# One index for four output rows: table columns in a new order, and a block's four slots in one buffer

## The chip, the cores and the metric

The kernel runs on one core of one Trainium2 chip. The time is the device time of one execution in microseconds (us). The kernel before took 394.58 us as the median of three runs (394.48 to 395.24).

## The reference

The input `x` has 8 sequences of 3072 rows with 256 values. A Fourier transform along the rows and one along the values is taken, and its real part goes through a maxout layer with three weight matrices and an output matrix:

```python
X = np.fft.fft(np.fft.fft(x, axis=1), axis=2).real      # (8, 3072, 256)
h = np.maximum(np.maximum(X @ w1, X @ w2), X @ w3)      # (24576, 768)
out = h @ w_out                                          # (24576, 256), float32
```

The real part at row k and at row 3072 - k consists of the same even and odd parts, added or subtracted. So a kernel can compute rows 0 to 1536 of a sequence and get the others, the mirror rows, from the same operands.

## The kernel before

The work goes in 8 batches, one for each sequence. A batch has two stages.

The first stage (class `Mix`) makes the two matrices `tE` and `tO`, 128 x 1536 each: the even and the odd part of the transform for 1536 output rows, one row of the output for each column. The input lies in `xt`, loaded by GpSimd's queue (`load_x`, L127; `fetch` in the plan) and mirrored (`mirror`). Method `s` transforms along 32 residues, `y` and `z` turn the result over through DRAM (stores of `tb` to `db`, loads of `yb`, both on SP's queue), and `k` (L461 to L471) multiplies with the tables `te_tab` and `to_tab`: one call for each table and each group of 512 columns. The columns of one call belong to several residues r of the row number modulo 32, and each residue needs its own weights (`col`). So a call is as many matmuls as the helper `_parts(g)` lists, 6 for groups 0 and 1 and 8 for group 2. The tables themselves are made once at the start: `ramp` and three more iotas write the row number of each column into `kvec`, and `phase`, `turns`, `wrap`, `angle` and `table` turn it into sines. `m.c` copies the first column of a few residues into `yb`. Row 0 of `tO` goes to DRAM and comes back to all 128 partitions as `vb` (`k` and `v`, SP's queue).

The second stage takes the 1536 columns as 3 blocks of 512 and, for each block, 6 units (one for each 128 of the 768 hidden values; 18 units a batch, 144 in all). A unit computes the three products for the direct rows (`begin`) and, by adding `gd_all` products on the same PSUM, for the mirror rows (`finish`, matmul L497), and takes their maximum into `hp` and `hm`. From unit 7 on, every odd unit is "split": its third product comes from `third` (L815 to L828), where VectorE makes `even` (L824), ScalarE makes `odd`, and GpSimd makes `plus` and `minus` (L828). VectorE's maximum in the split units (L837 for `plus`, L849 for `minus`) waits for these. `third` of a unit is issued one to two units ahead.

The output layer of a block (`l2_block`) runs beside the next block's units: ten matmuls of it are issued after each unit (`l2_some(10)`). A block has four slots of 128 columns. For each slot PE fills one PSUM bank `po` with the direct rows in its first half and the mirror rows in its second, and VectorE adds the even part and writes the 128 x 512 tile `ot` (L541). There are six such tiles. The column order is such that a slot's columns are consecutive values of j for one or two residues, with row number 32 j + r; a slot's direct rows are 32 apart, and `_runs(slot)` gives two or three runs of partitions that each go out with one store on SP's queue (L549), 1 KB a row. The mirror rows of a slot go out with one indexed store on GpSimd's queue (`scatter`, L622), one index and 1 KB a partition; slot 11 leaves out its first partition and stores 127 rows. A `memset` of one value follows each of them (L626). The indices `rows_m` (128 x 96) are made once by `rows`.

The last block of the last batch (`l2_last`) has flipped operands, so that its mirror rows too can leave with plain stores. It takes its slots in the order 3, 0, 1, 2, and after each slot its stores are dealt to ScalarE's, SP's and GpSimd's queues (L584). The row 1536 of all sequences comes from `l2_mid`.

Each engine takes its instructions in the order written here (the schedule is manual). The loop at the end of the kernel writes, for each unit: `finish` of the unit before if it is split, `begin`, `third`, `scatter`, `l2_some(10)`, then what the plan (`at`) holds for this unit. So on GpSimd's queue the indexed stores that have become ready stand between the `minus` of one `third` and the `plus` of the next.

Of the kernel before, what the change touches and what calls it, by code (L numbers as in the profile page):

```python
# [29 lines left out]
def _runs(slot):  # L30

    if slot == 11:
        return [(0, 48, 0), (48, 96, 16), (96, 128, 15 + 32 * 64)]
    t, u = divmod(slot, 3)
    edge, r = 96 - 32 * u, 4 * t + 1 + u
    return [(0, edge, r + 32 * 32 * u), (edge, 128, r + 1)]


def _parts(g):

    cols = [(r, 96 * (r - 1), 96 if r < 15 else 64, 0) for r in range(1, 16)]
    cols += [(0, 1408, 48, 0), (16, 1456, 48, 0), (15, 1504, 32, 64)]
    done = []
    for (r, c, wd, _) in cols:
        a, z = max(c, 512 * g), min(c + wd, 512 * g + 512)
        if a < z:
            done.append(((r - 1) % 16 if r < 16 else 16, a - 512 * g, z - a))
    return done
# [3 lines left out]
def kernel(  # L52
# [62 lines left out]
    rows_m = consts.tile([128, 12 * B], INT32, tag="rows_m")  # L115
# [50 lines left out]
    kvec = gen.tile([128, NHALF + 1], FP32, tag="kvec")  # L166
    kv = kvec[:, 0:1440].rearrange("p (r j) -> p r j", j=96)

    def ramp(r):
        n = {0: 6, 6: 5, 11: 4}[r]  # L170
        iota(kv[:, r:r + n, :], [[1, n], [32, 96]], base=r + 1)

    dvec = gen.tile([128, 128], FP32, tag="dvec")
    for c, (s0, s1) in enumerate(FIRST):
        for h in range(2):
            load_x(0, s0, s1, h)
        if c == 0:
            iota(dvec, [[1, 128]])
        elif c < 3:
            ramp((0, 6)[c - 1])  # L180
# [12 lines left out]
    ramp(11)  # L193
    iota(kvec[:, 1408:1504].rearrange("p (r j) -> p r j", r=2), [[16, 2], [32, 48]])
    iota(kvec[:, 1504:NHALF], [[32, 32]], base=15 + 32 * 64)
    iota(kvec[:, NHALF:NHALF + 1], [[0, 1]], base=NHALF)
# [72 lines left out]
    q = gen.tile([128, NHALF + 1], FP32, tag="q")  # L269
# [118 lines left out]
    class Mix:  # L388
# [72 lines left out]
        def k(self, which, g, evict=nc.scalar.copy):  # L461
# [3 lines left out]
            for (i, c0, wd) in _parts(g):  # L465
                nc.tensor.matmul(ps2[:, c0:c0 + wd], self.col(i, which),  # L466
                                 tab[:, g * 512 + c0:g * 512 + c0 + wd], start=True, stop=True)
# [42 lines left out]

    def l2_hidden(po, hcols):
        for jc in range(NJC):
            nc.tensor.matmul(po, hcols(jc), wout_bf[:, jc * 256:(jc + 1) * 256],  # L513
                             start=False, stop=(jc == NJC - 1), skip_group_check=True)
            yield

    def l2_block(b, blk, hp, hm, te, to):

        base = b * S
        for sub in range(4):  # L520
# [3 lines left out]
            if sub % 2 == 0:  # L524
# [10 lines left out]
            ot = out_pool.tile([128, 512], FP32, name="ot", tag="ot")  # L535
# [6 lines left out]
                out=ot.rearrange("p (h c) -> p h c", h=2),  # L542
                in0=po.rearrange("p (h c) -> p h c", h=2),
                in1=lin.unsqueeze(1).to_broadcast([128, 2, 256]), op=ALU.add)
            lo = 1 if slot == 11 else 0
            waiting.append((b * 12 + slot, lo, ot))
            for (p0, p1, k0) in _runs(slot):
                row = base + k0
                stored(nc.sync.dma_start(out=out[row: row + 32 * (p1 - p0 - 1) + 1: 32, :],  # L549
                                         in_=ot[p0:p1, 0:256]), "direct", ("scattered",))  # L550

    def l2_last(hp, hm, te, to, flipped):

        base = (B - 1) * S
        ter, tor = flipped
        for sub in (3, 0, 1, 2):
# [4 lines left out]
            ot = out_pool.tile([128, 512], FP32, name="ot", tag="ot")  # L561
            for (h, tev, tov, wo, hid) in (
                    (0, te[:, cp], to[:, cp], gw[:, 256:512], lambda jc: hp[:, jc, sp]),
                    (1, ter[:, sm], tor[:, sm], gw[:, 512:768], lambda jc: hm[:, jc, sm])):
                if h == 0 or sub == 2:
# [7 lines left out]
                if sub == 2:  # L573
                    nc.vector.tensor_copy(out=ot[:, h * 256:(h + 1) * 256], in_=ph)
            if sub != 2:
                nc.vector.tensor_copy(out=ot, in_=po)
            stores = [(p0, p1, base + k0, 0) for (p0, p1, k0) in _runs(slot)]
            for (p0, p1, k0) in _runs(slot):
                if k0 == 0:
                    p0, k0 = 1, 32  # L580
                stores.append((128 - p1, 128 - p0, base + S - k0 - 32 * (p1 - p0 - 1), 256))
            for k, (p0, p1, row, c) in enumerate(stores):
                eng = (nc.scalar, nc.sync, nc.gpsimd)[(k + (sub == 2)) % 3]
                stored(eng.dma_start(out=out[row: row + 32 * (p1 - p0 - 1) + 1: 32, :],  # L584
                                     in_=ot[p0:p1, c:c + 256]), "direct", ("scattered",))

    def l2_mid():
# [20 lines left out]
        for _ in l2_hidden(po[0:B, 0:256], lambda jc: hmid[:, jc, :]):  # L608
            pass
        ot = out_pool.tile([128, 512], FP32, name="ot", tag="ot")  # L610
        nc.vector.tensor_copy(out=ot[0:B, 0:256], in_=po[0:B, 0:256])
        stored(nc.sync.dma_start(out=out[NHALF: NHALF + S * (B - 1) + 1: S, :],
                                 in_=ot[0:B, 0:256]), "direct", ("scattered",))
# [4 lines left out]
    def scatter():  # L618

        while waiting:  # L620
            at_row, lo, ot = waiting.pop(0)
            stored(nc.gpsimd.indirect_dma_start(  # L622
                out, bass.IndirectOffsetOnAxis(
                    ap=rows_m[0:128 - lo, at_row: at_row + 1], axis=0),
                ot[lo:128, 256:512], None), "scattered", ("scattered", "direct"))
# [61 lines left out]
    m.c(1, 7)  # L687
# [9 lines left out]
    def rows():  # L697

        rows_f = gen.tile([128, 12 * B], FP32, tag="rows_f")
        iota(rows_f.rearrange("p (b t u) -> p b t u", t=4, u=3), [[S, B], [-4, 4], [-1025, 3]],  # L700
# [224 lines left out]
```

## Time and profile before

| | before |
|---|---|
| median of 3 runs | 394.58 us (394.48 to 395.24) |
| the profiled execution | 395.75 us, span 393.8 us |
| granted TensorE clock | 0.996 |
| TensorE (PE) busy | 377.7 us, 96% |
| VectorE (DVE) busy | 315.0 us, 80% |
| ScalarE (ACT) busy | 263.0 us, 67% |
| GpSimd (POOL) busy | 332.9 us, 85% |
| indexed stores L622 | 92, mean 1113 ns |
| DMA packets, bytes | 66901, 54.20 MB |

In the profile a line like "L622 POOL DMA_INDIRECT out_dram<-ot" names the line of the kernel, the engine, the operation, what is written and what is read. In the order of time the first two numbers are the start and the duration in us, and the brackets hold how long the engine was idle before and what released it. In the chain (the work that ended last, followed back) the numbers are start and length of a link. "issue" is time in which the engine waited for nothing that the profile shows. Matmuls overlap: each has some 0.16 us of latency, and the distance between starts is what a stream of them costs.

### The profile page before, as it was taken

To read this page: it belongs to the slowest core of one execution; us is meant where nothing else is said; L and a number is where in the kernel's file an instruction comes from. 1 tells how busy PE (TensorE), PEld (TensorE's weight loads), DVE (VectorE), ACT (ScalarE), POOL (GpSimd) and SP (SyncE) were. 2 spreads that over 40 slices of the span, in tenths; PEclk is the share of its full clock that TensorE was granted. 3 is DMA by queue.
4 is the path that set the end of the run, shared out by engine and by line. 5 is a ranking of instruction groups with operands and counts; after the bars stand their busy time and mean duration, and the time that the engine had idled before them with its cause. 6 is when DMAs were issued, how large, how long until landed. Compare 5 with 4: busy or idle time off the path is not lost.

```text
span 393.8 us, 8383 instructions
## 1 busy us (share of the span) xinstructions
PE 377.7 (96%) x2710; PEld 235.9 (60%) x2759; DVE 315.0 (80%) x530; ACT 263.0 (67%) x476; POOL 332.9 (85%) x432
## 2 busy tenths in 40 slices
PE   6698999999999999999999999999999999999994
PEld 2354566566665666565665666556665666666673
DVE  7788897788687788788787888877887887887972
ACT  6877788677766887577867787578866447435420
POOL 8985698979978899889988899889977898869993
PEclk9999999999999999999999999999999999999998
DMA  7999576585838776495767876495333553321234
GB/s 115 159 194 183 131 191 146 114 191 150 161 102 144 190 153 144 117 206 137 137 150 120 210 132 160 118 206 124 108 108 101 131 147 90 94 77 47 90 96 131
DMA packets 66901, 54.20 MB, mean 138 GB/s; under 512 B 32702, under 2 KB 62556, under 8 KB 66003
## 3 DMA queue, kind: packets, MB, share of 16 engines
q0 software_dynamic: 24368, 26.53, 35.5%
q1 hardware_dynamic: 41978, 26.72, 27.0%
q8 instruction: 21, 0.34, 0.4%
q10 hardware_dynamic: 512, 0.43, 0.4%
q14 instruction: 22, 0.18, 0.1%
HBM read 36.95 MB, written 30.81 MB: 172 GB/s over the span
## 4 chain that ended last, share of the span: by engine, by line
PE 84%; DMA 4%; DVE 4%; ACT 3%; issue 2%; POOL 2%; SPq 1%; DVEq 0%; ACTq 0%; POOLq 0%
PE po L513 30%; PE pse L497 12%; PE pse L490 8%; PE pse L491 7%; PE po L536 4%; PE d L821 4%; PE pse L835 4%; PE e L819 3%; PE ps L466 3%; PE pse L836 3%; PE pl L528 2%; PE ps L401 2%; DMA yb<-db 2%; DMA xt<-in_x_dram 2%; ACT tb L405 1%
## 5 line engine op out<-in xcount | busy, mean ns | idle before, releaser
L503 ACT ACTIVATE stmp<-pse 128x512 bf16<-128x512 f32 x150 | 89.6, 600 | 66.1 <-PE pse L497 50.9
L622 POOL DMA_INDIRECT out_dram<-ot,rows_m x92 | 102.4, 1113 | 17.9 <-issue 8.8
L828 POOL TENSOR_TENSOR plus<-even,odd 128x512 bf16<-128x512 f32 x69 | 87.8, 1272 | 32.9 <-DVE even L824 32.7
L828 POOL TENSOR_TENSOR minus<-even,odd 128x512 bf16<-128x512 f32 x69 | 87.5, 1268 | 0.0
L513 PE MATMUL po<-wout_bf,hp 128*128 128x256 bf16 x576 | 86.1, 273 | 0.4
L837 DVE SCALAR_TENSOR_TENSOR hp<-pse,plus 128x512 bf16<-128x512 f32 x69 | 47.6, 689 | 46.5 <-PE pse L836 13.9
L513 PE MATMUL po<-wout_bf,hm 128*128 128x256 bf16 x576 | 78.6, 273 | 0.0
L513 PEld LDWEIGHTS <-hp 128*128 128x128 bf16 x576 | 56.4, 98 | 26.1
L497 PE MATMUL pse<-tO,gd_all 128*128 128x512 bf16 x217 | 70.5, 379 | 1.1 <-DVE hp L504 0.2
L513 PEld LDWEIGHTS <-hm 128*128 128x128 bf16 x576 | 56.4, 98 | 16.3
L541 DVE TENSOR_TENSOR ot<-po,even 128x512 f32<-128x512 f32 x92 | 62.7, 681 | 0.0
L504 DVE TENSOR_TENSOR hp<-pse,stmp 128x512 bf16<-128x512 f32 x75 | 51.4, 685 | 10.1 <-ACT stmp L503 8.7
L490 PE MATMUL pse<-tE,g_all 128*128 128x512 bf16 x148 | 56.0, 379 | 1.9 <-DVE tE L468 0.5
L504 DVE TENSOR_TENSOR hm<-pse,stmp 128x512 bf16<-128x512 f32 x75 | 51.5, 687 | 7.4 <-ACT stmp L503 4.1
L824 DVE SCALAR_TENSOR_TENSOR even<-vb,wcol,e 128x512 f32<-128x512 bf16 x69 | 50.8, 737 | 0.0
L491 PE MATMUL pse<-tO,g_all 128*128 128x512 bf16 x131 | 49.6, 379 | 0.2 <-issue 0.2
L849 DVE SCALAR_TENSOR_TENSOR hm<-pse,minus 128x512 bf16<-128x512 f32 x69 | 47.0, 681 | 0.7
L823 ACT ACTIVATE odd<-d 128x512 f32<-128x512 f32 x69 | 41.3, 598 | 6.2
L134 ACT COPY xt<-xt 64x762 bf16<-64x762 bf16 (+1 forms) x48 | 40.2, 838 | 1.1
L497 PEld LDWEIGHTS <-gd_all 128*128 128x128 bf16 x219 | 21.3, 97 | 22.2 <-issue 4.1
L536 PE MATMUL po<-gw,tO 128*128 128x512 bf16 x85 | 32.3, 380 | 0.0
L405 ACT CAST tb<-ps 128x512 bf16<-128x512 f32 x38 | 20.5, 588 | 14.1 <-PE ps L401 14.1
(175 smaller groups left out, 475.7 us busy)
## 6 DMA issues: line engine op xcount, KB each, us to landing
xt<-in_x_dram POOLq DMA_DIRECT2D x14, 384.0 KB, 8.4
out_dram<-ot SPq DMA_DIRECT2D x55, 96.0 KB
out_dram<-ot SPq DMA_DIRECT2D x64, 64.0 KB
db<-tb SPq DMA_DIRECT2D x21, 192.0 KB
vb<-vd SPq DMA_DIRECT2D x23, 128.0 KB
xt<-in_x_dram POOLq DMA_DIRECT2D x7, 400.0 KB, 6.9
xt<-in_x_dram POOLq DMA_DIRECT2D x7, 368.0 KB, 6.1
out_dram<-ot SPq DMA_DIRECT2D x62, 32.0 KB
```

The costliest lines, as they stand in the source:

```text
L490: nc.tensor.matmul(pse[:, 0:n], g_all[:, jc, 2 * i, :], te, start=True, stop=False)
L491: nc.tensor.matmul(pse[:, 0:n], g_all[:, jc, 2 * i + 1, :], to, start=False, stop=True)
L497: nc.tensor.matmul(pse, gd_all[:, jc, i, :], to, start=False, stop=True, skip_group_check=True)
L503: nc.scalar.activation(out=stmp[:, 0:n], in_=pses[0][:, 0:n], func=AX.Relu)
L504: nc.vector.tensor_tensor(out=dst, in0=src3, in1=stmp[:, 0:n], op=ALU.max)
L513: nc.tensor.matmul(po, hcols(jc), wout_bf[:, jc * 256:(jc + 1) * 256], start=False, stop=(jc == NJC - 1), skip_group_check=True)
L536: nc.tensor.matmul(po, to[:, cp], gw[:, 256:768], start=True, stop=True)
L541: nc.vector.tensor_tensor(out=ot.rearrange("p (h c) -> p h c", h=2), in0=po.rearrange("p (h c) -> p h c", h=2), in1=lin.unsqueeze(1).to_br ...
L622: stored(nc.gpsimd.indirect_dma_start(out, bass.IndirectOffsetOnAxis(ap=rows_m[0:128 - lo, at_row: at_row + 1], axis=0), ot[lo:128, 256:51 ...
L824: nc.vector.scalar_tensor_tensor(out=even3, in0=vb, scalar=wcol[:, jc:jc + 1], in1=e3, op0=ALU.mult, op1=ALU.add)
L828: nc.gpsimd.tensor_tensor(out=dst, in0=even3, in1=odd3, op=op)
L837: nc.vector.scalar_tensor_tensor(out=dst, in0=pse2, scalar=0.0, in1=sums[g][0], op0=ALU.max, op1=ALU.max)
```

## The change

The columns of the tables get a new order. A block's four slots now hold four neighbouring residues on the same partition: in block 0, partition c below 96 of slot s holds row 32 c + 4 + s; in block 1 it holds 32 c + 8 + s; in block 2 it holds 32 c + 1 + s for three slots, and row 16 c + 16 in the fourth. Partitions 96 to 127 of every block hold rows 12 + s + 32 (c - 96) + 1024 times the block's number. So four direct rows of one partition are neighbours in the output. `_parts` follows: four pieces of 32 columns, and three or four of 96; in group 2 the fourth slot's 96 columns are two pieces of 48 that take every second column. Groups 0, 1 and 2 now have 8, 8 and 9 matmuls. `_runs` is gone.

A block's four slots go into one buffer of 128 x 8 x 256 values: the direct halves in places 0 to 3 and the mirror halves in places 7 to 4, so that the mirror rows too lie in the order of the output. There are three such buffers: the new `obuf`, and the two halves of `kq`, which holds `kvec` and `q` while the tables are made. The six `ot` tiles are gone.

When all four slots of a block are done, the direct rows leave with two stores on SP's queue in blocks 0 and 1 and three in block 2, up to 4 KB a partition. The mirror rows leave by one indexed store in blocks 0 and 1, of 4 KB for each of 128 indices, and by three in block 2: 96 indices of 3 KB, 32 of 4 KB and 95 of 1 KB. An index now counts groups of four rows, and an element offset gives the first row. `rows_m` has 5 columns, since the batch is in the offset.

`l2_last` takes its slots in the order 1, 2, 3, 0 and stores three of them together after the third, and the two halves of slot 0 as they come. `l2_mid` stores row 0 instead of row 1536 (that is now the column outside the blocks) and takes its tile from `even_pool`. `m.c(1, 7)` and `m.c(7, 16)` become one call before the first `k`; `rows` moves behind the plan's other entries of its unit group.

```diff
-def _runs(slot):
...
+FIRST_OF = (4, 8, 1)
 def _parts(g):
-    cols = [(r, 96 * (r - 1), 96 if r < 15 else 64, 0) for r in range(1, 16)]
-    cols += [(0, 1408, 48, 0), (16, 1456, 48, 0), (15, 1504, 32, 64)]
...
+    done = [(12 + i - 1, slice(128 * i + 96, 128 * i + 128)) for i in range(4)]
+    for i in range(4 if g < 2 else 3):
+        done.append((FIRST_OF[g] + i - 1, slice(128 * i, 128 * i + 96)))
+    if g == 2:
+        done += [(16, slice(384, 480, 2)), (15, slice(385, 480, 2))]
     return done
...
-    def ramp(r):
-        n = {0: 6, 6: 5, 11: 4}[r]
-        iota(kv[:, r:r + n, :], [[1, n], [32, 96]], base=r + 1)
+    def ramp(g):
+        kv = kvec[:, 512 * g:512 * g + 512].rearrange("p (s c) -> p s c", s=4)
+        n = 4 if g < 2 else 3
+        iota(kv[:, 0:n, 0:96], [[1, n], [32, 96]], base=FIRST_OF[g])
+        iota(kv[:, :, 96:128], [[1, 4], [32, 32]], base=12 + 1024 * g)
+        if g == 2:
+            iota(kv[:, 3, 0:96], [[16, 96]], base=16)
+            iota(kvec[:, NHALF:NHALF + 1], [[0, 1]], base=0)
...
+    obufs = [t.rearrange("p (f c) -> p f c", c=256)
+             for t in (obuf, kq[:, 0:2048], kq[:, 2048:4096])]
+    fours = out.rearrange("(n q) d -> n (q d)", q=4)
+    def stores_plus(b, blk, buf, s0=0, s1=4):
+        mine, v = rows_of(b)
+        r, n = FIRST_OF[blk], s1 if blk < 2 else min(s1, 3)
+        yield v[0:96, r + s0:r + n, :], buf[0:96, s0:n, :]
+        yield v[32 * blk:32 * blk + 32, 12 + s0:12 + s1, :], buf[96:128, s0:s1, :]
+        if n < s1:
+            yield mine[16:NHALF + 1:16, :], buf[0:96, 3, :]
+    def stores_minus(b, blk, buf):
+        flat = buf.rearrange("p f c -> p (f c)")
+        if blk < 2:
+            return [(b * S + 1, blk, 0, 128, flat[:, 1024:2048])]
+        return [(b * S + 1, 2, 0, 96, flat[0:96, 1280:2048]),
+                (b * S + 1, 3, 0, 32, flat[96:128, 1024:2048]),
+                (b * S, 4, 0, 95, flat[0:95, 1024:1280])]
...
     def l2_block(b, blk, hp, hm, te, to):
+        buf = obufs.pop(0)
+        obufs.append(buf)
...
             nc.vector.tensor_tensor(
-                out=ot.rearrange("p (h c) -> p h c", h=2),
+                out=buf[:, sub:8 - sub:7 - 2 * sub, :], in0=po.rearrange("p (h c) -> p h c", h=2),
...
-            waiting.append((b * 12 + slot, lo, ot))
-            for (p0, p1, k0) in _runs(slot):
...
+        for (dst, src) in stores_plus(b, blk, buf):
+            store(nc.sync, dst, src)
+        waiting.extend(stores_minus(b, blk, buf))
...
     def l2_last(hp, hm, te, to, flipped):
-        for sub in (3, 0, 1, 2):
+        for sub in (1, 2, 3, 0):
...
+                if sub == 0:
+                    nc.vector.tensor_copy(out=buf[:, 7 * h, :], in_=ph)
+                    stores = (stores_turned(B - 1, buf, 0, 1) if h else
+                              stores_plus(B - 1, 2, buf, 0, 1))
+                elif h:
+                    nc.vector.tensor_copy(out=buf[:, sub:8 - sub:7 - 2 * sub, :],
+                                          in_=po.rearrange("p (h c) -> p h c", h=2))
+                    if sub == 3:
+                        stores = [*stores_plus(B - 1, 2, buf, 1, 4),
+                                  *stores_turned(B - 1, buf, 1, 4)]
+                for k, (dst, src) in enumerate(stores):
+                    store((nc.scalar, nc.sync, nc.gpsimd)[k % 3], dst, src)
...
     def scatter():
         while waiting:
-            at_row, lo, ot = waiting.pop(0)
+            row, col, p0, p1, src = waiting.pop(0)
             stored(nc.gpsimd.indirect_dma_start(
-                out, bass.IndirectOffsetOnAxis(
-                    ap=rows_m[0:128 - lo, at_row: at_row + 1], axis=0),
-                ot[lo:128, 256:512], None), "scattered", ("scattered", "direct"))
+                fours, bass.IndirectOffsetOnAxis(ap=rows_m[p0:p1, col:col + 1], axis=0),
+                src, None, element_offset=256 * row), "scattered", ("scattered", "direct"))
             nc.gpsimd.memset(mark, 0.0)
```

More of the change, by code (lines that the diff above doesn't have):

```diff
@@ L464, in k @@
             ps2 = ps_f.tile([128, 512], FP32, name="ps2", tag="ps")
[L465 to L467 removed]
+            for (i, cols) in _parts(g):
+                nc.tensor.matmul(ps2[:, cols], self.col(i, which),
+                                 tab[:, g * 512:(g + 1) * 512][:, cols], start=True, stop=True)
             evict(out=(self.tE, self.tO)[which][:, g * 512:(g + 1) * 512], in_=ps2)
@@ L572, in l2_last @@
                 yield from l2_hidden(ph, hid)
[L573 to L585, printed above, removed]
+                stores = []
+                if sub == 0:
[10 more added lines that the diff above has]
+                    store((nc.scalar, nc.sync, nc.gpsimd)[k % 3], dst, src)
     def l2_mid():
@@ L775 @@
                     (3, lambda: m.c(16, RI)), (3, lambda: m.c(0, 1)),
-                    (3, lambda: table(2)), (3, lambda: table(0)), (5, rows),
+                    (3, lambda: table(2)), (3, lambda: table(0)),
                     (4, lambda: m.k(1, 2)), (4, lambda: m.k(0, 2)), (4, m.end),
-                    (5, column), (5, lambda: next(second)), (6, lambda: m.v(2))):
+                    (5, rows), (5, column), (5, lambda: next(second)), (6, lambda: m.v(2))):
         at(0, u, fn)
```

85 lines of the change are left out of this document (32 added, 53 removed).

## The prediction

> **What bounds the kernel now.** I read the page's shares and chain, then busy time by stretch, then the order of POOL, DVE and PE at the place where PE stops, then the tail. All sums are against the profiled execution (395.75 us: a span of 393.8 and 1.95 around it). It is 1.17 us above the median of 394.58; I take the differences over to the median.
>
> From the page, engines and the chain's shares by engine, then busy time by stretch (length; PE, PEld, DVE, ACT, POOL; granted clock, DMA share, GB/s):
>
> ```profile
> PE 377.7 (96%) x2710; PEld 235.9 (60%) x2759; DVE 315.0 (80%) x530; ACT 263.0 (67%) x476; POOL 332.9 (85%) x432
> ...
> PE 84%; DMA 4%; DVE 4%; ACT 3%; issue 2%; POOL 2%; SPq 1%; DVEq 0%; ACTq 0%; POOLq 0%
> ```
> ```profile
> 150.00:200.00 50.00, 49.63 (x364) 31.42 (x370) 40.62 (x64) 36.50 (x65) 44.55 (x55) 1.00 0.72 154
> ```
>
> PE is busy 49.63 of 50 us, so the middle is PE-bound. A batch takes 44.92 us (the same line of the chain starts at 150.07 and at 194.99). Work taken from POOL, SP or the DMA engines pays only where it closes PE's holes: about 0.35 us a batch. Anything added to PE counts in full.
>
> Where are those holes? POOL and DVE in order of time in the third batch (start, duration), then the chain over the same stretch:
>
> ```profile
> 134.04 2.55 POOL L622 DMA_INDIRECT out_dram<-ot,rows_m  x1 [0.22 <-DVE hm L504]
> ...
> 136.63 1.28 POOL L828 TENSOR_TENSOR plus<-even,odd 128x512 bf16<-128x512 f32 x1
> ```
> ```profile
> 137.95 0.69 DVE L837 SCALAR_TENSOR_TENSOR hp<-pse,plus 128x512 bf16<-128x512 f32 x1 [1.64 <-PE pl L528]
> ```
> ```profile
> 138.79 0.28 PE pse L497
> ...
> 140.59 0.35 PE po L536
> ...
> 141.16 0.36 PE pse L835
> ```
>
> POOL issues two mirror scatters, of slot 10 (at 132.75, 0.98 us) and slot 11 (the line at 134.04). The second has 127 rows instead of 128 and takes 2.55 us. The sum `plus` (L828) stands behind it and starts at 136.63, although its operand `even` was ready at 134.5. DVE's maximum L837 starts 0.04 us after `plus` ends at 137.91 (not `pl`, done long before). From then on DVE is late, and PE loses 0.06 us at L497 (0.28 for 0.22), 0.13 at L536 and 0.14 at L835: 0.33 us, nearly the whole hole of a batch. The 2.55 us scatter occurs 7 times, once a batch from 88.34 to 358.26.
>
> **The change, part by part.**
>
> *Table columns (added on PE).* `_parts` cuts each table's three groups into 8, 8 and 9 matmuls instead of 6, 6 and 8: 25 for 20, two tables, 8 batches, so 80 matmuls more over the same columns. Prices from the chain:
>
> ```profile
> 35.24 0.58 PE psc L356 x24
> ...
> 148.53 0.47 PE ps L466 x12
> ```
>
> One-column matmuls cost 0.58/24 = 24 ns. Six of the present groups 0 and 1 (mostly 96 columns) cost 0.235, eight of group 2 0.25 (at 111.30). With 25 ns up to 48 columns and 42 ns for 96 (40 at 2.4 columns a ns, plus the 2 ns by which 256 columns, 109 ns, exceed 106.7), these give 0.235 and 0.25 for the old cuts and for the new 4x25+4x42 = 0.268, twice, and 4x25+3x42+2x25 = 0.276: +0.033, +0.033 and +0.026, or 0.092 a table, x16 = **+1.5 us**, with nothing to hide it. No row shows a moving operand of stride 2, as the two 48-column pieces have. Below: 25 ns as for 48 contiguous columns. Above: half rate, 40 ns, 32 such pieces, +0.5. I take zero (the reads lie within one row of the table); the +0.5 goes into the range.
>
> Weighed against this: the Trainium skill, "TensorE: Matmul & The Clock Gate", section "Back-to-back issue gap", gives a roofline of 81 ns a matmul at 128 columns for streams with weight loads, which for 80 more would be an estimated +6.5 us; its table also gives a floor of about 25 ns up to 64 columns, and that one the 24 ns here agree with.
>
> *Scatters (POOL, the disputed term).* 92 indexed stores of 1 KB rows become 37 of rows up to 4 KB: one for each of blocks 0 and 1, three for block 2. In the changed program those three stand where slots 10 and 11 stood, behind the same `minus` and ahead of the same `plus`. So the price is the length of that chain. Now, from 132.75 to 136.63: 0.98 + 2.55 and 0.35 of marks and gaps. After: three scatters of 96, 32 and 95 rows, with three marks (0.09) and two gaps (0.22), 0.71. It breaks even where the three sum to 3.17. 128 rows cost 0.98; I take 0.95 and 0.90 for 96 and 32 (fewer rows; direct stores of 32 and of 96 rows cost 0.50 to 0.57 and 0.52, so rows cost little). Longer rows: the 384 to 400 KB loads of x, 12 KB a partition, issue in 0.56 to 0.79, so bytes cost POOL next to nothing. For 95 rows the ends are 0.98 and 2.55. Which is nearer? The two scatters side by side land very differently, the 128-row one of 132.75 after 6.6 us, the 127-row one after twice that:
>
> ```profile
> L622 POOL DMA_INDIRECT out_dram<-ot,rows_m x1: 2547/2547/2547, 134.0 to 134.0; - x1
> ...
> DMA to landing us min/median/max: 12.7/12.7/12.7
> ```
>
> 127 is prime and 128 divides by 16; slow issue and late landing fit 127 rows falling on one of the 16 DMA engines. If the share is the largest divisor up to 16, 95 rows go on five engines, 19 each. Issue then runs from 0.98 (8 rows an engine) to 2.55 (127), 13 ns a row: 19 rows, 1.12. The three sum to 2.97, and `plus` starts 0.20 earlier. Of the 0.33 us hole that leaves about 0.1 (L497's 0.06 and most of the other two go): 7 x 0.22 = **-1.5 us**. The ends: hole closed, -2.3; 95 rows at 2.55, `plus` 1.23 later, which PE pays in full since L497 is already late, +8.6.
>
> The rule behind this is in the Trainium skill, "DMA: Bandwidth & Descriptors", section "Why a DMA increments its semaphore by 16 and not by 1": the largest k up to 16 that divides both sides, 127 on one engine; the 12.7 us landing agrees, and no row shows 95.
>
> Elsewhere fewer scatters save POOL some 55 x 1.3 us, worth nothing: there PE has no hole.
>
> *Stores on SP.* 198 stores become 58. Now block 2's last slot, slot 0's stores and the second pair of `yb` loads queue in turn; in the changed program block 2's three stores come first and all four `yb` loads follow. Against that, 512 KB instead of 128 KB lie just ahead of the loads, about 1.5 us at 250 to 300 GB/s. In batch 2 alone the loads are late (the chain):
>
> ```profile
> 91.80 7.90 DMA yb<-db
> ```
>
> SP reached them late (1.5 us in L549 before), ACT (L455, at 99.88) waited 1.4 us for them and PE lost 0.46 of the 10 us from 100 (9.54 busy). Issued about 4 us earlier and 1.5 later in the queue, they land in time: **-0.4 us** (ends -0.5 and 0). What was late next there is ACT's own chain.
>
> *Start.* The two ramps before the last loads of x become a 4x96 and a 4x32 iota each. By rows: 0.483 (384 elements) + 0.274 (128) = 0.757, against 0.684 and 0.608: +0.22 on POOL. The load it delays lands at 13.48 with the DMA engines 0.9 busy, so between 0 and +0.22 reaches the chain: **+0.1**. One copy of column 0 instead of two (`m.c`) hides behind the `te` matmuls; `rows` shrinks where POOL idles 5.34 us before its first `plus`: nothing.
>
> *Tail.* PE's and DVE's work is the same, but the stores of three of the last four slots now leave together after the third copy.
>
> ```profile
> 388.00:389.00 1.00, 0.42 (x4) 0.13 (x2) 0.42 (x1) 0.00 (x0) 0.70 (x2) 1.00 0.75 212
> ...
> 390.00:391.00 1.00, 0.00 (x0) 0.00 (x0) 0.00 (x0) 0.00 (x0) 0.00 (x0) 0.86 0.77 196
> 391.00:392.00 1.00, 0.00 (x0) 0.00 (x0) 0.00 (x0) 0.00 (x0) 0.00 (x0) 0.50 0.03 6
> ```
>
> Data flows until 391.1 now. 768 KB from about 388.5 and 256 KB more, at 300 GB/s (212 at a share of 0.75 gives 283), end near 391.9: +0.8. But SP's last store, now issued at 389.5 (it waited for an earlier store), can go at 388.9: -0.6. **+0.3**, ends -0.6 and +0.8.
>
> *DVE's evictions* keep count and size (92 at 681 ns); the three buffers come round after three blocks (45 us), the longest landing is 12.8: nothing.
>
> Sum: 1.5 - 1.5 - 0.4 + 0.1 + 0.3 = 0.0. Forecast **394.6 us**, no change that can be told (what a measurement here tells from no change is about 0.2%, 0.8 us).
>
> **Rivals.**
> 1. *The 95-row scatter is slow like the 127-row one.* For it: 95 is no multiple of 16. Against: it has a divisor that 127 lacks. From 1.25 us on it decides (then the chain is 0.07 shorter than now at most and 1.5 us of matmuls stand nearly uncovered); 1.6 us gives `plus` 0.28 later, 7 x 0.28 = +2.0 in place of -1.5: 398.1; in proportion to rows (0.98 + 1.57x95/127 = 2.15), 402; the end, 404.7.
> 2. *The matmuls stand and the holes stay*: three scatters and 512 KB at once delay something else (the trio slower through 4 KB rows, `vb`, or the tail). For it: 1 MB now leaves at each block's end, 3.4 us of the DMA engines. Against: shares of 0.4 to 0.7. 394.6 + 1.5 + 0.4 = 396.5.
> 3. *Faster.* The 32- and 95-row scatters cost under 0.8 each, `plus` starts 0.6 to 0.7 earlier, holes close (-2.3), `yb` -0.5, tail -0.4, k +1.5: 392.9. For it: PE's lost time is all behind POOL there. Against: 0.96 is the least of 92 scatters.
> 4. *Weight loads show.* At 32 columns the load (97 ns each in `yb`'s row) might not be covered: 80 x 97 = 7.8 instead of 1.5, 400.9. The 24 ns row speaks against it. The Trainium skill's 81 ns roofline would be a case of this.
> That the rows do not leave as 4 KB packets would change DMA shares, not PE: no case of its own.
>
> **How the numbers follow.** Forecast 0.38 (own range 393.8 to 395.4); rival 1 0.22, 2 0.17, 3 0.20, 4 0.03. Same 0.38, faster 0.20 (rival 3), slower 0.42. The range, 392.8 to 400.0, leaves out rival 1's upper half, rival 4 and the rim of rival 3, below 0.2.
>
> **What would show it.** L466's runs at 0.27 us for 8; the third scatter of block 2 near 1.1 us and `plus` 0.2 earlier behind `minus`; L497 and L835 without their extra 0.06 and 0.14; no `yb` in the chain near 90; data ending by 391.9 in the tail. The 95-row scatter's length is what would make it wrong most.

## The result, and the profile after

The changed kernel takes 395.77 us (median of 19 runs, 395.07 to 396.18), the kernel before on the same chip 394.98 us (median of 19, 394.48 to 395.96). The ratio is 1.0017, with a 95% interval of 1.0010 to 1.0024. That is a loss of about 0.7 us, which lies under the 0.2% from which on the prediction calls a change one that can be told. The profiled execution of the changed kernel took 395.28 us with a span of 393.5 us. That is at the low end of its runs, while the profile of before (395.75 us) is at the high end of its own. The two profiles therefore differ by less than the medians and with the other sign, and the lines below are compared stage by stage and not by their ends.

The page: engines' busy time, then the chain's shares by engine.

```profile
PE 381.8 (97%) x2839; PEld 238.5 (61%) x2839; DVE 315.5 (80%) x530; ACT 263.1 (67%) x475; POOL 260.2 (66%) x319
...
PE 90%; DVE 3%; POOL 2%; DMA 2%; ACT 1%; issue 1%; DVEq 0%; POOLq 0%
```

POOL lost 73 us of work and the time did not follow: 90% of the chain is PE (84% in the profile of before, 88% in a second profile of it, experiment 6). Busy time by stretch (length; PE, PEld, DVE, ACT, POOL; clock, DMA share, GB/s), of the changed kernel and then of the kernel before in its second profile:

```profile
150.00:200.00 50.00, 50.00 (x383) 31.64 (x381) 40.58 (x64) 36.41 (x65) 33.48 (x38) 1.00 0.65 153
150.00:200.00 50.00, 50.00 (x370) 31.32 (x368) 40.65 (x64) 36.37 (x64) 44.57 (x54) 1.00 0.73 154
```

PE is busy all the time in both, and the 50 us hold 383 matmuls instead of 370, where the new cuts add ten a batch. So the busy share does not show the holes at all: the records of neighbouring matmuls overlap by some 0.16 us, pauses of 0.06 to 0.14 us vanish in that, and a hole appears only as longer links in the chain. The 49.63 us of the first profile of before, with 364 matmuls, are seven breaks of some 53 ns where records are missing (2710 matmuls recorded in all, 2759 in the second profile).

POOL in order of time at the place of the old hole, in the third batch (start, duration):

```profile
132.35 0.99 POOL L649 DMA_INDIRECT out_dram<-kq,rows_m  x1 [0.17 <-issue]
...
133.64 0.90 POOL L649 DMA_INDIRECT out_dram<-kq,rows_m  x1 [0.22 <-issue]
...
134.84 1.13 POOL L649 DMA_INDIRECT out_dram<-kq,rows_m  x1 [0.23 <-DVE obuf L574]
...
136.03 1.27 POOL L843 TENSOR_TENSOR plus<-even,odd 128x512 bf16<-128x512 f32 x1
```

The three scatters of block 2 have 96, 32 and 95 rows. They take 0.99, 0.90 and 1.13 us where the prediction took 0.95, 0.90 and 1.12, and `plus` starts 3.68 us behind the first of them, where it was 3.88 in the kernel before. VectorE's maximum and PE's chain behind it:

```profile
137.33 0.69 DVE L852 SCALAR_TENSOR_TENSOR hp<-pse,plus 128x512 bf16<-128x512 f32 x1 [1.45 <-POOL plus L843]
```
```profile
138.37 0.22 PE pse L491
...
140.10 0.22 PE po L569
...
140.54 0.36 PE pse L850
```

L491 (before: L497, 0.28) and L569 (before: L536, 0.35) run at their plain 0.22. Only L850 (before: L835, 0.36) still carries 0.14 us: of the 0.33 us hole 0.14 is left.

The table of what follows. "Batch" is the mean of four batches, between the starts of the same line of the chain (the one near 149.5 and the one near 329). "Last group" is the start of the last run of ten `po` matmuls in the chain, and "end behind it" is what the span still had from there.

| kernel | ratio to before [95%] | batch, us | last group | end behind it |
|---|---|---|---|---|
| before | 1 | 44.92 | 380.06 | 13.7 |
| changed | 1.0017 [1.0010, 1.0024] | 44.95 | 379.53 | 14.0 |
| before, new cut count (cuts_alone) | 1.0036 [1.0022, 1.0049] | 45.11 | 380.95 | 13.8 |
| changed, old cuts (cuts_undone) | 0.9959 [0.9945, 0.9973] | 44.69 | 378.01 | 13.9 |
| changed, 96 indices (scat96) | 0.9985 [0.9976, 0.9994] | 44.83 | 378.97 | 13.7 |
| before, 128 indices (slot11_128) | 1.0004 [0.9995, 1.0013] | 44.56 | 377.02 | 16.7 |
| before, 112 indices (slot11_112) | 1.0002 [0.9992, 1.0011] | 44.56 | 376.97 | 16.6 |
| changed, contiguous pieces (plain48) | 1.0041 [1.0026, 1.0055] | 44.90 | 379.26 | 15.3 |
| changed, contiguous and 96 (both) | 1.0035 [1.0023, 1.0047] | 44.76 | 379.19 | 15.2 |
| the same, 47-row store cut (both_split) | 0.9988 [0.9977, 1.0000] | 44.76 | 378.54 | 14.3 |
| the same, last stores not on POOL (both_nopool) | 0.9968 [0.9955, 0.9980] | 44.76 | 378.06 | 13.2 |
| changed, 89 indices (scat89) | 1.0151 [1.0132, 1.0169] | 45.87 | 386.34 | 13.2 |
| before, 128 indices, last stores not on POOL (slot11_nopool) | 0.9921 [0.9907, 0.9935] | 44.56 | 376.40 | 13.3 |

The start of a single execution varies: the first such group of the chain begins between 51.6 and 53.0 us, and it differs by up to 1.1 us among kernels whose start is the same code. So a last group that is some tenths of a us apart says nothing; the batch does.

### The profile page after: what moved, and what is told of

Read it like the earlier page. It is cut to its first block, busy times and chain, and to the rows that moved or that the text cites. A ratio compares the mean times of both kernels' runs of the same rounds, so it can differ in the third digit from the quotient of the medians.

```text
span 393.5 us, 8107 instructions
## 1 busy us (share of the span) xinstructions
PE 381.8 (97%) x2839; PEld 238.5 (61%) x2839; DVE 315.5 (80%) x530; ACT 263.1 (67%) x475; POOL 260.2 (66%) x319
## 4 chain that ended last, share of the span: by engine, by line
PE 90%; DVE 3%; POOL 2%; DMA 2%; ACT 1%; issue 1%; DVEq 0%; POOLq 0%
PE po L546 31%; PE pse L491 12%; PE pse L484 8%; PE pse L485 8%; PE po L569 5%; PE pse L850 4%; PE pse L851 4%; PE e L834 4%; PE d L836 4%; PE ps L460 3%; PE ps L395 3%; PE pl L562 2%; DMA xt<-in_x_dram 2%; POOL xt L120 1%; DVE yb L428 1%
## 5 line engine op out<-in xcount | busy, mean ns | idle before, releaser
L497 ACT ACTIVATE stmp<-pse 128x512 bf16<-128x512 f32 x150 | 89.6, 600 | 64.8 <-PE pse L491 39.8
L491 PE MATMUL pse<-tO,gd_all 128*128 128x512 bf16 x219 | 70.9, 380 | 0.0
L484 PE MATMUL pse<-tE,g_all 128*128 128x512 bf16 x150 | 56.8, 379 | 0.8 <-DVE tE L462 0.4
L485 PE MATMUL pse<-tO,g_all 128*128 128x512 bf16 x150 | 56.8, 379 | 0.0
L498 DVE TENSOR_TENSOR hm<-pse,stmp 128x512 bf16<-128x512 f32 x75 | 51.6, 688 | 6.4 <-ACT stmp L497 2.5
L574 DVE TENSOR_TENSOR kq<-po,even 128x512 f32<-128x512 f32 x60 | 40.9, 682 | 0.0
L569 PE MATMUL po<-gw,tO 128*128 128x512 bf16 x92 | 34.9, 379 | 0.0
L491 PEld LDWEIGHTS <-gd_all 128*128 128x128 bf16 x219 | 21.4, 98 | 22.1 <-issue 4.1
L649 POOL DMA_INDIRECT out_dram<-kq,rows_m x29 | 28.9, 996 | 7.5 <-issue 2.9
```

The lines of the kernel that those rows point to most:

```text
L484: nc.tensor.matmul(pse[:, 0:n], g_all[:, jc, 2 * i, :], te, start=True, stop=False)
L485: nc.tensor.matmul(pse[:, 0:n], g_all[:, jc, 2 * i + 1, :], to, start=False, stop=True)
L491: nc.tensor.matmul(pse, gd_all[:, jc, i, :], to, start=False, stop=True, skip_group_check=True)
L497: nc.scalar.activation(out=stmp[:, 0:n], in_=pses[0][:, 0:n], func=AX.Relu)
L498: nc.vector.tensor_tensor(out=dst, in0=src3, in1=stmp[:, 0:n], op=ALU.max)
L569: nc.tensor.matmul(po, to[:, cp], gw[:, 256:768], start=True, stop=True)
```

## The experiments

**1. The cuts alone, and everything but the cuts.** The theory: the changed kernel is the sum of the predicted terms, above all +1.5 us of matmuls against -1.5 us of holes. The rival: the new scatters and loads gave nothing, and what is seen is the cuts at half their price. The kernel before with only the number of cuts raised, pieces of 32 columns that stay contiguous:

```
             done.append(((r - 1) % 16 if r < 16 else 16, a - 512 * g, z - a))
+    for at in ((0,), (5, 0), (4,))[g]:
+        i, c, wd = done.pop(at)
+        done += [(i, c + k, 32) for k in range(0, wd, 32)]
     return done
```

> The kernel before with nothing changed but the cuts: a 96-column and the 64-column pieces of each table are split so that groups 0, 1 and 2 have 8, 8 and 9 matmuls of the changed kernel's widths (none with stride 2). Theory A (the prediction's terms: cuts +1.5, scatters -1.5, loads of yb -0.4, start +0.1, tail +0.3): +1.5 us on before, ratio 1.0037, with the holes at L497, L536 and L835 of each batch still there. Rival B (scatters and loads gave nothing, and the measured +0.7 us of the change is all that the cuts cost): +0.7 us, ratio 1.0017.

And the changed kernel with the old table of cuts in `_parts` (the values of `tE` and `tO` do not fit the new column order then):

> The changed kernel with the old cuts of 6, 6 and 8 matmuls over the new columns. Their weights then belong to the wrong residues, so the values of tE and tO are wrong; all shapes, stores and waits are the changed kernel's. A: 1.5 us below the changed kernel, that is 0.7 to 0.8 us below before (ratio about 0.998). B: as before, ratio 1.000.

Measured: 396.72 us, ratio 1.0036, for the cuts alone, as the theory had it; a batch is 0.19 us longer, x8 = 1.5 us. Without them the changed kernel takes 393.56 us, ratio 0.9959. The rival falls: the other parts together gain 1.6 us against before, and a batch is 0.23 us shorter. But taking the cuts out of the changed kernel gains 0.58%, or 2.3 us, where putting them into the kernel before cost 1.4; by the batches it is 0.26 us against 0.19, or 2.1 us against 1.5 in all. The difference shows in the chain (start, length) of the changed kernel, then of the kernel before with the new count:

```profile
63.09 0.27 PE ps L460 x8
65.53 0.31 PE ps L460 x9
```
```profile
63.36 0.26 PE ps L469 x8
65.80 0.27 PE ps L469 x9
```

Eight matmuls cost the same in both, 0.26 to 0.27 as predicted. The nine of group 2 cost 0.31 in the changed kernel and 0.27 where all pieces are contiguous. Group 2 is the one with the two pieces of 48 columns that take every second column. Two such groups a batch at 0.04 us each give 0.6 us in all, as the batches do; the rest of the difference between 2.3 and 1.4 is within the intervals.

**2. The stride.** The changed kernel with these two pieces contiguous; cosine argument, mirror index and direct stores of that quarter follow.

```
-        done += [(16, slice(384, 480, 2)), (15, slice(385, 480, 2))]
+        done += [(16, slice(384, 432)), (15, slice(432, 480))]
...
-            yield mine[16:NHALF + 1:16, :], buf[0:96, 3, :]
+            yield v[0:48, 16, :], buf[0:48, 3, :]
+            yield v[1:49, 0, :], buf[48:96, 3, :]
...
-            yield mine[NHALF + 16:S - 15:16, :], buf[33:128, 4, :]
+            yield v[48:96, 16, :], buf[80:128, 4, :]
+            yield v[49:96, 0, :], buf[33:80, 4, :]
```

> The changed kernel with the two 48-column pieces of group 2 contiguous instead of every second column: columns 384 to 431 from slot 16, 432 to 479 from slot 15. The cosine argument, the mirror index and the direct stores of that quarter follow (rows 32j+16 and 32j+32 as two stores of 48 partitions), so there is one direct store more a batch and nothing else changes. Theory A now (the stride costs what the chain shows: nine matmuls of group 2 in 0.31 us where contiguous cuts took 0.27): x9 back at 0.27, 16 tables x 0.04 = 0.64 us, so 395.1 against the changed kernel's 395.8 and a ratio to the kernel before of 1.0001. Rival B (the 0.31 is only how the modelled ends fall, PE's pace does not depend on the stride): as the changed kernel, 1.0017.

The chain of that kernel, then its groups of 48-column matmuls (count, busy and mean ns of one); the last fence is the same group in the changed kernel:

```profile
65.63 0.28 PE ps L460 x9
```
```profile
L460 PE MATMUL ps<-to_tab,yb 128*128 128x48 bf16 x16 | 1.7, 184 | 0.0
```
```profile
L460 PE MATMUL ps<-to_tab,yb 128*128 128x48 bf16 x16 | 2.0, 212 | 0.0
```

The stride lengthens the record of such a matmul by 28 ns. What counts is the distance between starts, since matmuls overlap: 0.03 us per nine by the chain, or 15 ns for each of the two pieces, and 0.05 us a batch by the table, so 0.4 to 0.5 us in all. The time nevertheless went up, to 396.81 us and a ratio of 1.0041 instead of 1.0001. It was lost behind PE's work: the end comes 15.3 us behind the last group instead of 14.0. The DMA engines of that kernel at the end, by stretch:

```profile
390.00:391.00 1.00, 0.00 (x0) 0.00 (x0) 0.00 (x0) 0.00 (x0) 0.00 (x0) 0.50 0.71 209
391.00:392.00 1.00, 0.00 (x0) 0.00 (x0) 0.00 (x0) 0.00 (x0) 0.00 (x0) 0.50 0.08 26
392.00:393.00 1.00, 0.00 (x0) 0.00 (x0) 0.00 (x0) 0.00 (x0) 0.00 (x0) 0.50 0.07 23
```

A share of 0.07 is one engine of 16. The experiment brought in a store that the changed kernel does not have: 47 rows of 1 KB on SP's queue in the last batch, and 47 is prime like 127. SP waited 2.8 us for that landing at the end. That it is this store is tested in experiment 3.

**3. Contiguous pieces and 96 indices; then the 47 rows cut.** First the 96 indices alone: the third scatter takes row 1536 from the mirror half, and the direct store gives it up.

```
-                (b * S, 4, 0, 95, flat[0:95, 1024:1280])]
+                (b * S, 4, 0, 96, flat[0:96, 1024:1280])]
...
-            yield mine[16:NHALF + 1:16, :], buf[0:96, 3, :]
+            e = 96 if b == B - 1 else 95
+            yield mine[16:16 * e + 1:16, :], buf[0:e, 3, :]
```

> The changed kernel with 96 indices instead of 95 in the third scatter of block 2 (it then also writes row 1536, from the mirror half, and the direct store gives up that row: 95 instead of 96 partitions on SP's queue). A: the third scatter takes 0.99 instead of 1.13 us, plus starts 0.14 earlier, the hole of 0.14 us that is left in front of L850 closes, seven times: 1.0 us below the changed kernel, ratio to before about 0.999. B: no change against the changed kernel, 1.0017 to before.

Measured 394.59 us, ratio 0.9985. POOL and the chain at the place of the hole in the third batch:

```profile
134.95 0.92 POOL L650 DMA_INDIRECT out_dram<-kq,rows_m  x1 [0.23 <-DVE obuf L575]
```
```profile
140.67 0.22 PE pse L851
```

The third scatter takes 0.92 instead of 1.13, and the 0.14 us that was left of the hole is gone; a batch is 0.12 us shorter. This one index makes the changed kernel faster than the kernel before, by 0.15%.

With the contiguous pieces as well:

> The contiguous pieces together with 96 indices in the third scatter (row 1536 from the mirror half; the 47 direct rows that are left as stores of 32 and 15 partitions, except in the last batch). If the two are independent, the ratio of 0.9985 that 96 indices alone gave falls by another 0.0016: 0.9969, 393.8 us. If the stride is free (rival B): 0.9985.

Measured 396.37 us, ratio 1.0035. The batch is 44.76, another 0.07 shorter, so on PE the two add up; the end has the 47-row store again (SP waits 3.0 us for it). With that store cut into 32 and 15 rows:

```
-            yield v[49:96, 0, :], buf[33:80, 4, :]
+            yield v[49:81, 0, :], buf[33:65, 4, :]
+            yield v[81:96, 0, :], buf[65:80, 4, :]
```

> The version with contiguous pieces and 96 indices, where the last batch's direct store of 47 rows (one DMA engine, on which SP waited 3.0 us at the end) is cut into 32 and 15 rows. Theory A (the time lost by the two contiguous versions was that store alone): no single engine left busy after 392 us, the span ends about 13.7 us after the start of the last group of the chain, as with 96 indices alone; 394.2 us, ratio 0.9975. Rival (contiguous pieces cost elsewhere): 1.0035 again.

Measured 394.33 us, ratio 0.9988. The single engine is gone:

```profile
391.00:392.00 1.00, 0.00 (x0) 0.00 (x0) 0.00 (x0) 0.00 (x0) 0.00 (x0) 0.76 0.00 0
```

The end is 0.9 us closer to the last group than with the 47-row store, but with 14.3 us still 0.6 farther than with 96 indices alone, so the 0.4 us by which PE is ahead there does not show in the time. The reason stands in POOL's queue. The three slots of the last block that are stored together leave with nine stores where the changed kernel has six, and as they are dealt to three queues, POOL gets three of them instead of two. The instruction DRAIN at the end of POOL's queue (experiment 5) comes behind them; here it is for this version and then for 96 indices alone (minimum, median and maximum of the durations in ns; first and last start):

```profile
L944 POOLq DRAIN  x3: 46/103/5005, 387.0 to 392.5; - x3
```
```profile
L936 POOLq DRAIN  x3: 46/103/4920, 387.0 to 392.4; - x3
```

Although PE was earlier, the drain starts at the same 387.0 and ends at 392.0 against 391.9. SP has its last landing before that, at 391.6 and 391.3. So it is POOL's queue that holds the end here; the version without stores on it follows in experiment 5.

**4. What the share of an engine costs.** The changed kernel with 89 indices in the third scatter, a prime below 95.

```
-                (b * S, 4, 0, 95, flat[0:95, 1024:1280])]
+                (b * S, 4, 0, 89, flat[0:89, 1024:1280])]
```

> The changed kernel with 89 indices in the third scatter (89 is prime; the mirror rows of 6 partitions a batch are left out). Theory A (the number of engines is the largest divisor up to 16, and POOL takes 13 ns for each row of an engine's share): 89 rows on one engine, 0.98 + 0.0132 x 81 = 2.05 us instead of 1.13, plus 0.92 us later, and PE, which has no slack there any more, pays in full: 7 x 0.92 = +6.4 us, 402.2, ratio 1.018. Rival (the time goes by the number of rows, or 95 was slow for another reason): 1.1 us, as the changed kernel, ratio 1.0017.

Measured 401.28 us, ratio 1.0151. POOL, then the chain of the third batch:

```profile
136.12 2.05 POOL L649 DMA_INDIRECT out_dram<-kq,rows_m  x1 [0.22 <-DVE obuf L574]
```
```profile
136.12 2.05 POOL out_dram L649
138.17 0.09 POOL mark L652
138.25 1.26 POOL plus L843
```

Six rows fewer than 95, and 0.92 us longer: 2.05 us, to the second decimal what 13 ns for each row of one engine's share gives. With 96 rows at 0.92 (6 a share), 95 at 1.13 (19), 89 at 2.05 (89) and 127 at 2.55 (127), the time goes by rows over the largest divisor up to 16, and not by rows. (The rows of a share, in brackets, are worked out by this rule; the trace shows the times.) The landing goes the same way, 5.8 us after the issue with 96 rows, 10.1 with 89 and 12.7 with 127. Now the scatter and `plus` are on the chain themselves. Compared with the changed kernel the last group comes 6.8 us later, of which 0.4 is there already at the start of the second stage: 6.4, the expected 7 x 0.92. The ratio stayed below the expected 1.018 and the time below 402.2 us, since the end follows 0.8 us sooner.

**5. The hole without the new layout.** The kernel before with 128 indices for slot 11: row 0 comes from the mirror half, and the direct store starts at partition 1.

```
-            lo = 1 if slot == 11 else 0
+            lo = 0
...
+                if k0 == 0:
+                    p0, k0 = 1, 32
```

> The kernel before with 128 instead of 127 indices in slot 11's scatter (it then also writes row 0 of the sequence from the mirror half, and the direct store gives up that row: 47 instead of 48 partitions on SP's queue); the columns, the cuts and all else as before. A: this scatter takes 0.98 instead of 2.55 us, plus starts up to 1.57 earlier, the hole of 0.33 us closes seven times: -2.3 us, ratio 0.994. B: the holes are not the scatter's, ratio 1.000.

The scatter takes 0.97 us, `plus` follows directly, and the batch is 44.56 us:

```profile
133.13 0.97 POOL L624 DMA_INDIRECT out_dram<-ot,rows_m  x1 [0.22 <-DVE hm L504]
...
134.15 1.27 POOL L833 TENSOR_TENSOR plus<-even,odd 128x512 bf16<-128x512 f32 x1
```

That is 0.36 us a batch less, 2.5 us over seven: the hole is gone. PE ends 3.0 us sooner than in the first profile of before and 2.4 us sooner than in the second, which lacks an accident of the first (experiment 6). And the time is 395.39, ratio 1.0004, not the 0.994 expected. So the end of the program, after PE, took the gain back. The instructions of the last line of the kernel (queue and operation; minimum, median and maximum of their durations in ns; first and last start) for this version, then for the kernel before:

```profile
L925 POOLq DRAIN  x3: 46/103/7760, 385.2 to 393.4; - x3
L925 SPq DRAIN  x3: 7/7/7, 389.2 to 393.2; - x3
```
```profile
L920 POOLq DRAIN  x3: 46/103/4820, 388.2 to 393.5; - x3
L920 SPq DRAIN  x3: 7/7/7, 391.9 to 393.3; - x3
```

SP has its last landing by 389.2, 2.7 us sooner than before. But POOL's queue goes through a drain, an instruction whose record begins as POOL issues its last store; it lasted 7.76 us here and 4.82 before, and both end at 393.0. The last semaphores of all other queues come behind it, from 393.1 on. Two readings were open: a peculiarity of this version, or something in POOL's queue that sets the end of the kernel before as well. The second version takes 112 indices:

> The kernel before with 112 indices instead of 127 in slot 11's mirror scatter: the mirror rows of partitions 113 to 127 are left out (15 rows a batch are not written), the direct stores stay as they were. With 128 indices PE ended 3.0 us earlier and the time did not move, because POOL's last drain took 7.8 us instead of 4.8. Theory A (the holes are worth 0.33 us x 7 and more, and the long drain was a peculiarity of that version): scatter near 0.98, PE's last matmul near 385.4, drain near 4.9, 392.2 us, ratio 0.9935. Rival C (whatever the drain waits for is there always and ends near 393 us of the span, so that POOL's queue and not PE sets the end of the kernel before): PE as early, drain near 7.8, ratio 1.000.

Measured 395.45 us, ratio 1.0002, batch 44.56, drain 7.68 us. It is no peculiarity of one version. So the third one takes POOL out of the last block's direct stores:

```
-                eng = (nc.scalar, nc.sync, nc.gpsimd)[(k + (sub == 2)) % 3]
+                eng = (nc.scalar, nc.sync)[(k + (sub == 2)) % 2]
```

> The kernel before with 128 indices in slot 11's scatter and without POOL in the last block's direct stores. Theory D (the 7.8 us drain belongs to POOL's direct stores): PE ends near 385.8 as before, last landing near 389.5, end about 390.4 of the span, 392.3 us, ratio 0.9925. Rival E (the drain waits for something of the scatters, or of the whole program's descriptors): POOL's drain still ends near 393, ratio 1.000.

Measured 391.71 us, ratio 0.9921, 3.3 us below the kernel before and the fastest of all. The drain:

```profile
L925 POOLq DRAIN  x3: 46/97/8022, 379.4 to 389.4; - x3
L925 SPq DRAIN  x3: 7/7/7, 388.9 to 389.2; - x3
```

The drain is as long as ever, 8.02 us. But it starts at 379.4, next to the last scatter (issued at 379.6), and is over at 387.4, before SP has its last landing at 388.9. So the time came as theory D had it, but its reason did not hold: without any direct store on POOL the drain is no shorter. That settles what set the end of the version with 128 indices (the moment at which POOL issues its last transfer, plus the drain). For the kernel before it rests on the trace alone, where the drain ends at 393.0 and SP's last landing is at 391.9. Why a drain lasts 4.1 us (89 indices), 4.8 (before), 5.2 (changed) or 8.0 stays open: the trace does not show what it waits for.

The same edit in the contiguous version with 96 indices:

> The same with the last block's direct stores on ScalarE's and SyncE's queues only, none on POOL. In the changed kernel SP had all landings at 392.0 and POOL's last drain ended at 392.75. Theory D (POOL's drain sets the end, and it is long because of its direct stores): POOL's drain starts after its last scatter near 382 and is over before the last landing; the end comes 0.5 us earlier than with POOL: 393.7 us, ratio 0.9962. Rival (the last landing sets the end, and two queues are slower than three): no gain, 0.9975 to 0.999.

Measured 393.59 us, ratio 0.9968: the end comes 13.2 us behind the last group instead of 14.3. The drain is 6.1 us long, against 5.0 with direct stores on POOL, so here too they are not what makes it long. It is the fastest version with the new layout and its cuts, and 1.9 us behind the old layout with one more index. Most of that is the 80 matmuls (a batch of 44.76 against 44.56, x8 = 1.6).

**6. The kernel before once more.** The late loads of `yb` in batch 2 were a term of the sum, but the kernels of experiments 1 (the cuts alone) and 5 have the same program on SP, some of them but for one row of a store, and did not show them.

> The kernel before once more, for a second profile. Theory A (the late yb loads of batch 2 belong to the program): the wait of 7.9 us for yb near 92 and PE's gap of 0.46 us are there again. Rival (they were that one execution's, since the versions with the same SP program did not show them): no yb in the chain near 92, batch 2 about 0.5 us shorter.

Measured 395.06 us, span 393.1. The chain around 92, where the first profile had the 7.90 us of `yb`:

```profile
91.20 0.43 PE pse L497 x2
91.64 0.21 PE e L819
91.85 0.22 PE d L821
```

PE runs through; no load is waited for, and the last group comes 0.7 us sooner than in the first profile (379.37 against 380.06). The 7.90 us were that execution's and not the program's, and with them most of the 0.46 us that PE lacked from 100 to 110.

## Why the prediction was right, and where it was not

**The case.** The forecast was no change that can be told, 394.6 us with an own range of 393.8 to 395.4 against a kernel before of 394.58. The measured ratio of 1.0017 puts it at 395.25 on that scale: the case that had the largest single chance, near the upper end of its own range, 0.7 us above the sum of 0.0. That the two large terms, cuts and scatters, cancel was forecast with the right mechanism and is no luck; that the misses of the others still left the time inside the case was close. The terms one by one:

*Table columns, +1.5 us: right for the contiguous part, wrong for the stride.* The cuts alone measured +1.4 us (ratio 1.0036) and 0.19 us a batch, against 0.092 a table and two tables. The 0.27 us for eight is in the chain to the digit. The step that failed is "I take zero (the reads lie within one row of the table)" for the pieces of stride 2. They cost 0.4 to 0.5 us by the batches of experiments 2 and 3, the upper end (+0.5, at 40 ns a piece instead of 25) that was given and not taken. That step looked only at the operand that is read. The same slice also addresses the output in PSUM, which is written at every second value. The Trainium skill, "PSUM — Partial Sum Buffer", section "Specifications (TRN2)", names cachelines of 8 bytes and says that any access that is not contiguous slows matmuls significantly; two float32 values fill such a line. The trace agrees in sign, with 28 ns on a matmul of 48 columns. No run here separates the stride of the write from that of the read.

*Scatters, -1.5 us: right, with its mechanism.* Scatter times 0.99, 0.90 and 1.13 against 0.95, 0.90 and 1.12, `plus` 0.20 earlier, 0.14 of the hole left where about 0.1 was expected. Everything but the cuts gains 0.23 us a batch (cuts_undone against before), 1.6 us over seven. The size of the hole was right (0.33 us by the links of the chain, 0.36 a batch in experiment 5), but one of the two readings behind it was not: the 0.35 us a batch drawn from 49.63 busy us of 50 were breaks at missing records, and that this number agreed with the chain's was chance. Rival 1, whose question was the 95-row scatter, falls with the line of 1.13 us, and 89 rows show what it was about: a scatter of 2.05 us and a ratio of 1.0151, with the linear price of 13 ns a row of the share that the prediction had drawn between 8 and 127 rows.

*Stores on SP, -0.4 us: wrong.* The step took the late `yb` loads for a property of batch 2. The second profile of the kernel before does not have them, nor do the two versions with exactly its program on SP (cuts_alone and slot11_112). There was nothing to gain. No `yb` in the chain near 90 was named as a sign that the prediction is right; it came true without telling anything, as the kernel before does not have it either in its second profile. The first profiled execution lay 1.17 us above the median, and this wait was a part of that; a wait that occurs in one batch of eight should have been taken for an accident first, with 0 (one of the ends given) as its value.

*Start, +0.1:* not to be told apart; executions with the same start differ by more than that. *Tail, +0.3:* the size was right (5.15 us from VectorE's last copy to the end of the span, 4.92 before) and the mechanism was not. Data was to end by 391.9; it ended near 391.1 (DMA's share is 0.01 from 391 to 392), and the end came at 393.5 all the same. SP's first drain, behind its last landing, begins at 392.0, POOL's drain ends at 392.75. By the trace POOL's queue set the end, and the prediction had only data in view, although the profile of before has 2.7 us between the end of data and the end of the span.

In place of 1.5 - 1.5 - 0.4 + 0.1 + 0.3 the runs give 1.5 + 0.45 - 1.6 + 0 + 0 + 0.2 = 0.55 of the 0.7 that were measured. Two of the misses, the stride and `yb`, have the same sign.

*The rivals.* Rival 2 (the matmuls stand, the holes stay) is refuted by the chain and by the 393.56 us without the cuts, although its time of 396.5 was only 1.2 us off. Rival 3 (faster) needed scatters under 0.8 us; the least was 0.86. Rival 4 (weight loads show) would have been 7.8 us; with 0.19 us a batch nothing of it is there.

## What to carry to other kernels

Where one engine is busy throughout, removing another engine's work pays only what it closes of the first one's holes: here 73 us of POOL's work were worth 1.6 us, and one more index (128 instead of 127) closed the same hole without the 80 matmuls that the new layout needs. Count the rows of a transfer by their largest divisor up to 16, for the time that POOL takes to issue it as well as for its landing. Before a term is taken from a wait in a profile, see whether it repeats from batch to batch and in a second profile, and whether records are missing; and look behind the last data for what the program waits for, since some 2.4 us won earlier stayed invisible there until POOL's last stores were given to other queues.

## What was not expected of the hardware

- A float32 output in PSUM with stride 2 and a table read with stride 2 made the record of a 48-column matmul 212 ns long instead of 184, and a run of nine with two of them 0.31 us instead of 0.28.
- POOL's drain at the end of the program lasts 4.1 to 8.0 us, counted from about the issue of POOL's last transfer, whether that is a direct store or a scatter. In versions that differ from the kernel before in little but 15 rows fewer or one row more in one scatter a batch it was 7.7 and 7.8 us instead of 4.8, which took back all that PE had won. What it waits for stays open.
- The time that POOL takes to issue an indexed store went by rows over the largest divisor up to 16: 0.92 us for 96 rows, 1.13 for 95, 2.05 for 89 and 2.55 for 127, some 13 ns for each row of a share.
- One direct store of 47 rows on SP's queue kept a single DMA engine busy (a share of 0.07) after all others had finished, and SP waited 2.8 and 3.0 us for it.
